# Attention and a routed expert layer: block rows issued two steps ahead, the first two blocks turned by TensorE, q's norms as a row

## The chip, the cores and the metric

One core of a Trainium2 chip runs the whole program. The metric is device time in microseconds (us) of one execution, taken as the median of several runs. A separate execution was recorded by the hardware profiler; its page and trace are what the argument reads. Engines: TensorE (PE, with its weight load PEld), VectorE (DVE), ScalarE (ACT), GpSimd (POOL) and SyncE (SP). SP and POOL each issue DMAs from a queue of their own, in order.

## The reference

Four batches of 5056 tokens with 256 channels go through an attention over channels, and all 20224 tokens then through a layer of eight experts of which each token takes one. The core of it:

```python
qn = q / (np.linalg.norm(q, axis=1, keepdims=True) + 1e-06)     # q, k, v: [4, 5056, 256]
kn = k / (np.linalg.norm(k, axis=1, keepdims=True) + 1e-06)
s = kn.transpose(0, 2, 1) @ qn / tau                             # [4, 256, 256]
a = softmax(s)                                                   # along the last axis
x = (v @ a).reshape(20224, 256)

logits = x @ w_gate + modality_bias[modality_id]                 # 8 experts
e_idx = argmax(logits); gate_w = softmax(logits)[e_idx]
for e in range(8):
    mask = e_idx == e
    out[mask] = gate_w[mask, None] * (np.maximum(x[mask] @ w1[e], 0) @ w2[e])   # 256 -> 1024 -> 256
```

The norms run over the tokens, one for each channel. Which expert a token goes to is known only on the chip.

## The kernel before

The program goes through 40 steps (`g`, ten for each batch, 512 tokens each; the last of a batch has 448) and 40 blocks (`slot`, up to 512 tokens of one expert each).

*Scores.* `kq_pieces` (line 265) loads q and k of a step and adds up k^T q in two PSUM tiles (`g0`, `g1`). The squares of q and k go by ScalarE, and VectorE adds them into `acc`, in two halves of 512 columns (line 347). Batch 0 is done ahead of everything; the pieces of the next batch run among the steps of the present one.

*Softmax.* `norms` (line 401), once in each batch, sums the squares over the partitions: eight products with a column of ones (line 409), which give the norms as columns. ScalarE takes the root, VectorE adds 1e-6 and takes the reciprocal. Those of k scale rows, so a column serves (`rk`). Those of q scale columns and are needed as a row in each partition: VectorE scales a unit matrix by them (`dq`), and a product with ones (line 435) spreads the row into PSUM (`rq`). `soft` then scales, takes the exponential and normalizes, and `turn_weights` and `gate_weights` make the weights `ah`, `al` that a step multiplies v with.

*Steps.* `va_pieces` (line 568) turns v, multiplies (`xp`, line 633), routes (`route`, line 639) and scatters the 512 rows into a table `xs` in device memory, ordered by expert, with four indirect DMAs of POOL's queue (line 529). Each row has its channels, its gate and its token's number.

*Blocks.* After a step, `pick` chooses an expert with a full block of rows. `block_pieces` (line 771) has what is to be done for it: `load_x` (line 777) reads the first row's number and fetches the rows (`xr`) by four DMAs of POOL's queue, a quarter of the channels each, in runs of 64 numbers, and the gates and numbers (`gt`) by a fifth. They depend on all scatters up to the step after which the block was chosen. `load_w` fetches the expert's weights in two halves, by SP's queue; `split_w` splits them, in four parts, into a rounded part and the rest (ScalarE's copy, VectorE's difference). `tr_x` (line 840) turns the rows: VectorE transposes squares of 32x32 (line 563), which with the order of the four quarters gives the whole turn, and then rows are split in the same way into `xh` and `xl`. `m1` (`hp`, line 861), a relu (`hh`, `hl`), `m2` (`y`, line 879) and `finish` (`yo`) follow, and four indirect DMAs of POOL scatter the results (line 529).

*Order.* The pieces of a step, of a block and of the next batch's scores are interleaved by `_interleave` (line 20), and a scheduler then sets each engine's order by its own estimate; the engines carry it out in that order. In the main loop (line 1012) a block chosen after step `gg` runs at `g` where `gg <= g - lag(g)`, with a lag of 4 that falls to 3; its loads (rows and weights together, the pieces under `"load"`) are issued at the start of the step before, and its rows are turned and its first weights split (`"prep"`) in the latter half of the block before. Block 0 is the first to run, at step 6. The rows' tiles have two buffers, the weights' three.

## Time and profile before

| | |
|---|---|
| time, median of 3 runs | 1216.53 us (1212.48 to 1221.39) |
| the profiled execution's own time | 1214.25 us |
| its span, first to last instruction | 1212.6 us |
| TensorE busy | 1175.0 us, 97% |
| VectorE, ScalarE, GpSimd busy | 879.8, 730.1 and 508.8 us |
| mean granted clock of TensorE | 0.986 |
| moved by DMA | 210.78 MB, 174 GB/s |

The profile's page gives busy time by engine, forty slices of the span with TensorE's granted clock, groups of instructions by line, and DMA issues. Its trace answers questions about single stretches. In a row of a timeline stand the start in us, the length in us, engine, line, operation, output<-inputs and count; a bracket tells how long the engine was idle before it and what ended that ("issue": nothing that the profile shows). In a row of windows stand the stretch, its length, the busy time of PE, PEld, DVE, ACT and POOL, the granted clock, the DMA engines' busy share and GB/s. A time of 1 us is 0.08% of the whole.

### The profile page before, as it was taken

Reading aid. Unit: us, or ns where it says so; the run is one execution under the profiler, and the core shown is the slowest. Engines: PE = TensorE matmul, PEld = TensorE weight load, DVE = VectorE, ACT = ScalarE, POOL = GpSimd, SP = SyncE. Lnnn points to the kernel's source line nnn. Section 1 sums busy time; section 2 is a strip of 40 time slices with the busy share of each in tenths; the row PEclk is TensorE's granted clock in tenths of the full one; section 3 lists DMA queues with packets and bytes.
Section 4 is the critical chain, followed back from the end, with each engine's and each line's share of the span. In section 5 each row is a group of like instructions: output and inputs, shape, how many; then the busy total and the mean of one; then the engine's idle time right before and its main releaser. Section 6 shows DMA issues by size and latency. Waiting matters only on the chain.

```text
span 1212.6 us, 22887 instructions
## 1 busy us (share of the span) xinstructions
PE 1175.0 (97%) x7654; PEld 1065.2 (88%) x7654; DVE 879.8 (73%) x2199; ACT 730.1 (60%) x1447; POOL 508.8 (42%) x544
## 2 busy tenths in 40 slices
PE   9996998999999999999989998999999999999997
PEld 8985987899999998998879997999999999999997
DVE  5697788887777877877678877766676677676552
ACT  6674586866666666676556665556555555554553
POOL 0057454325344444444434444333445344555432
PEclk9998998999999999999989998999999999999999
DMA  8977687557555666655656665554556554555430
GB/s 310 327 241 190 194 228 196 170 175 209 173 175 166 185 185 189 178 169 173 176 143 192 186 174 155 155 142 136 148 154 182 162 171 124 147 161 152 117 112 29
DMA packets 172399, 210.78 MB, mean 174 GB/s; under 512 B 80584, under 2 KB 126152, under 8 KB 172272
## 3 DMA queue, kind: packets, MB, share of 16 engines
q1 hardware_dynamic: 147632, 146.75, 41.7%
q0 software_dynamic: 24640, 62.49, 17.0%
q8 instruction: 62, 1.02, 0.4%
q14 instruction: 65, 0.53, 0.1%
HBM read 167.06 MB, written 43.43 MB: 174 GB/s over the span
## 4 chain that ended last, share of the span: by engine, by line
PE 44%; issue 3%; DVE 1%; DMA 1%; POOL 1%; POOLq 0%; ACT 0%; DVEq 0%; ACTq 0%
PE y L879 19%; PE hp L861 19%; PE xp L633 4%; PE g L370 1%; DMA xr<-xs 1%; PE g L374 1%; POOL out_dram L529 0%; DMA gt<-xs 0%; DVE hl L865 0%; DVE vt L563 0%; DVE w1l L836 0%; PE ns L409 0%; DVE xt L563 0%; PE rp L672 0%; POOLq L1062 0%
## 5 line engine op out<-in xcount | busy, mean ns | idle before, releaser
L529 POOL DMA_INDIRECT xs<-x,pi x160 | 184.9, 1155 | 463.1 <-ACT w1h L829 138.6
L879 PE MATMUL y<-w2h,hh 128*128 128x256 f32 x1264 | 357.6, 283 | 0.6 <-ACT yo L894 0.6
L879 PE MATMUL y<-w2l,hh 128*128 128x256 f32 x1264 | 354.9, 281 | 0.0
L879 PE MATMUL y<-w2h,hl 128*128 128x256 f32 x1264 | 352.9, 279 | 0.1
L861 PE MATMUL hp<-xh,w1h 128*128 128x512 f32 (+1 forms) x640 | 251.3, 393 | 3.4 <-DVE hl L865 3.4
L861 PE MATMUL hp<-xl,w1h 128*128 128x512 f32 (+1 forms) x640 | 253.3, 396 | 0.0
L865 DVE SCALAR_TENSOR_TENSOR hl<-hp,hh 128x512 fp32r<-128x512 f32 (+1 forms) x320 | 216.9, 678 | 50.2 <-ACT hh L864 49.2
L861 PE MATMUL hp<-xh,w1l 128*128 128x512 f32 (+1 forms) x640 | 251.8, 393 | 0.0
L879 PEld LDWEIGHTS y<-w2h,hh 128*128 128x128 f32 x1264 | 239.0, 189 | 13.5 <-ACT yo L894 1.0
L879 PEld LDWEIGHTS y<-w2l,hh 128*128 128x128 f32 x1264 | 239.4, 189 | 10.7
L864 ACT ACTIVATE hh<-hp 128x512 fp32r<-128x512 f32 (+1 forms) x320 | 189.6, 592 | 85.2 <-PE hp L861 76.5
L879 PEld LDWEIGHTS y<-w2h,hl 128*128 128x128 f32 x1264 | 238.2, 188 | 1.3 <-issue 0.9
L529 POOL DMA_INDIRECT out_dram<-yo,gt x158 | 172.2, 1090 | 149.6 <-ACT yo L894 106.3
L836 DVE TENSOR_TENSOR w1l<-w1r,w1h 128x512 fp32r<-128x512 f32 x160 | 110.2, 689 | 132.4 <-ACT w1h L829 132.4
L829 ACT CAST w1h<-w1r 128x512 fp32r<-128x512 f32 x160 | 99.2, 620 | 155.6 <-PE hp L861 155.3
L861 PEld LDWEIGHTS hp<-xh,w1l 128*128 128x128 f32 x640 | 121.2, 189 | 28.2 <-issue 2.9
L836 DVE TENSOR_TENSOR w2l<-w2r,w2h 128x512 fp32r<-128x512 f32 x160 | 110.1, 688 | 48.5 <-ACT w2h L829 45.9
L861 PEld LDWEIGHTS hp<-xl,w1h 128*128 128x128 f32 x640 | 121.3, 190 | 17.8 <-issue 4.2
L861 PEld LDWEIGHTS hp<-xh,w1h 128*128 128x128 f32 x640 | 121.1, 189 | 17.5 <-DVE hl L865 3.8
L783 POOL DMA_DIRECT2D xr<-xs x160 | 107.5, 690 | 52.6 <-DMA xs<-x,pi 22.2
L829 ACT CAST w2h<-w2r 128x512 fp32r<-128x512 f32 x160 | 100.5, 629 | 42.1 <-PE y L879 42.1
L633 PE MATMUL xp<-ah,vh 128*128 128x264 f32 x320 | 92.5, 289 | 2.1 <-DVE vl L610 1.0
(158 smaller groups left out, 1804.1 us busy)
## 6 DMA issues: line engine op xcount, KB each, us to landing
w1r<-in_moe_w_dram SPq DMA_DIRECT2D x80, 512.0 KB, 4.8
w2r<-in_moe_w_dram SPq DMA_DIRECT2D x80, 512.0 KB, 6.0
xr<-xs POOLq DMA_DIRECT2D x152, 128.0 KB, 3.6
q<-in_q_dram SPq DMA_DIRECT2D x35, 512.0 KB, 4.2
k<-in_k_dram SPq DMA_DIRECT2D x35, 512.0 KB, 5.3
v<-in_v_dram SPq DMA_DIRECT2D x112, 128.0 KB, 6.0
v<-in_v_dram SPq DMA_DIRECT2D x8, 512.0 KB, 10.3
xs<-x,pi POOLq DMA_INDIRECT x160, 3.6
```

The source lines that it names most:

```text
L370: nc.tensor.matmul(g, ks[:pp, t, m * P : (m + 1) * P], qs[:pp, t, :], start=first, stop=False, skip_group_check=True,)
L374: nc.tensor.matmul(g[:, 0:C], ks[:pp, t, C + m * P : C + (m + 1) * P], qs[:pp, t, 0:C], start=False, stop=last, skip_group_check=True,)
L529: ins = nc.gpsimd.indirect_dma_start(out=dst, out_offset=bass.IndirectOffsetOnAxis(ap=idx, axis=0), in_=rows, in_offset=None, bounds_check ...
L633: nc.tensor.matmul(xp[:, 0:DE], a[:, h, t * P : (t + 1) * P], w[:, h, :], start=i == 0, stop=i == len(seq) - 1,)
L783: nc.gpsimd.dma_start(xr[j * Q : (j + 1) * Q, 0 : rows // Q, :], src[:, j * CQ : (j + 1) * CQ].rearrange("(i t) c -> t i c", t=Q),)
L829: ins = nc.scalar.copy(hi, src).ins
L836: nc.vector.tensor_tensor(lo, src, hi.bitcast(F32), ALU.subtract)
L861: nc.tensor.matmul(hp[:, 0:rows], w[:, h, fs], x[:, h, 0:rows], start=i == 0, stop=i == len(seq) - 1)
L864: nc.scalar.activation(hh[:, 0:rows], hp[:, 0:rows], AF.Relu)
L865: nc.vector.scalar_tensor_tensor(hl[:, 0:rows], hp[:, 0:rows], 0.0, hh[:, 0:rows].bitcast(F32), ALU.max, ALU.subtract)
L879: ins = nc.tensor.matmul(y, a[:, tsl], w[:, j % 2, :], start=(j == 0 and i == 0 and t % 2 == 0), stop=(j == NJ - 1 and i == 2), skip_group ...
```

## The change

Four things are changed.

1. A block's rows are a piece of their own (`"rows"`, apart from `"load"`), issued up to two steps ahead of the block's run instead of one, after the first blocks. For block 0 they stand between the two halves of its weights.
2. The rows of blocks 0 and 1 (`WHOLE_ROWS`) are fetched by one DMA of SP's queue, whole rows of 256 numbers, with the gates by a second.
3. TensorE turns the rows of these two blocks by products with a unit matrix (`identr`, `xtp`), one PSUM tile for each half of the channels; ScalarE and VectorE split them from there. The other blocks are turned by VectorE as before.
4. `norms` adds the halves of `acc` first (VectorE). One product of a full matrix of ones with q's sums gives them as a row in every partition, and two small products give k's as columns, into the same tile. Root, 1e-6 and reciprocal run over all 258 columns; the scaled unit matrix and its product are gone.

```diff
-            ns = ps2.tile([P, 512], F32, tag="aux", name=f"ns_{b}")
-            for m in cols:
-                for h in range(2):
-                    cs = slice(m * P, (m + 1) * P) if m < CH else slice(C + m - CH, 2 * C, CH)
-                    nc.tensor.matmul(
-                        ns[:, m : m + 1], a[:, h, cs], ones[:, 0:1],
-                        start=m == cols[0] and h == 0, stop=h == 1, skip_group_check=True,
-                    )
...
-            dq = p1.tile([P, CH, P], F32, tag="at", name=f"dq_{b}")
-            for m in range(CH):
-                nc.vector.tensor_scalar(dq[:, m, :], ident, inv[:, m : m + 1], None, ALU.mult)
-            rq = ps2.tile([P, 512], F32, tag="aux", name=f"rq_{b}")
-            nc.tensor.matmul(rq[:, 0:C], ones, dq.rearrange("p m c -> p (m c)"), start=True, stop=True)
-            st["rq"] = rq
+            nc.vector.tensor_tensor(a[:, 0, :], a[:, 0, :], a[:, 1, :], ALU.add)
+            W = C + CH
+            ns = ps2.tile([P, 512], F32, tag="aux", name=f"ns_{b}")
+            nc.tensor.matmul(ns[:, 0:C], ones, a[:, 0, 0:C], start=True, stop=True, skip_group_check=True)
+            for m in range(CH):
+                nc.tensor.matmul(
+                    ns[:, C + m : C + m + 1], a[:, 0, C + m : 2 * C : CH], ones[:, 0:1],
+                    start=False, stop=True, skip_group_check=True,
+                )
+            inv = p1.tile([P, W], F32, tag="at", name=f"inv_{b}")
+            root = nc.scalar.activation(inv, ns[:, 0:W], AF.Sqrt).ins
...
+            st["rq"] = inv
...
-            r = nc.gpsimd.value_load(pki[0:1, 0:1], min_val=0, max_val=E * CAP)
-            xr = st["xr"] = p2.tile([P, QI, CQ], F32, tag="xr", name=f"xr_{slot}")
+            eng = nc.sync if slot < WHOLE_ROWS else nc.gpsimd
+            r = eng.value_load(pki[0:1, 0:1], min_val=0, max_val=E * CAP)
+            if slot < WHOLE_ROWS:
+                xr = p2.tile([P, TT, D], F32R, tag="xr", name=f"xr_{slot}")
+            else:
+                xr = p2.tile([P, QI, CQ], F32, tag="xr", name=f"xr_{slot}")
...
+                eng.dma_start(xr[:, 0:tt, :].bitcast(F32), src[:, 0:D].rearrange("(t p) c -> p t c", p=P))
+            ] if slot < WHOLE_ROWS else [
...
+            if slot < WHOLE_ROWS:
+                tp = ps2.tile([P, 512], F32R, tag="aux", name=f"xtp_{slot}_{h}")
+                for t in range(tt):
+                    nc.tensor.matmul(
+                        tp[:, t * P : (t + 1) * P], st["xr"][:, t, h::CH], identr,
+                        is_transpose=True, start=t == 0, stop=True, skip_group_check=True,
+                    )
+                raw, hi, lo = tp[:, 0:rows].bitcast(F32), xh[:, h, 0:rows], xl[:, h, 0:rows]
...
-        prep = [load_x, lambda: load_w(0), lambda: load_w(1)]
+        prep = [lambda: load_w(0), lambda: load_w(1)]
+        ahead = [load_x]
         if slot == 0:
 
-            prep[0:2] = reversed(prep[0:2])
-        prep2 = [lambda: split_w(0), tr_x, lambda: None, lambda: split_w(1)]
+            prep, ahead = prep[:1] + ahead + prep[1:], []
+        prep2 = [lambda: split_w(0), lambda: tr_x(0), lambda: tr_x(1), lambda: split_w(1)]
...
         for gg, blk in waiting:
+            n = 2 if g > first_block + WHOLE_ROWS else 1
+            if gg <= g + n - lag(g + n):
+                once(blk, "rows")
+        for gg, blk in waiting:
             if gg <= g + 1 - lag(g + 1):
                 once(blk, "load")
```

Since a scheduler sets the orders, the diff alone does not tell where the instructions stand. In the rows below a name is followed by its block or step, and then by a buffer's number; `pki` is the block's choice, of which the first row's number is read.

The first place is SP's queue at the first two blocks. Before:

```order
L806 DMA w1r_0_0_1179<-in_moe_w1_dram 128x2x512
L810 DMA w2r_0_0_1180<-in_moe_w2_dram 128x4x256
L806 DMA w1r_0_1_1199<-in_moe_w1_dram 128x2x512
L810 DMA w2r_0_1_1200<-in_moe_w2_dram 128x4x256
L802 TENSOR_LOAD pki_1_1028
L806 DMA w1r_1_0_1371<-in_moe_w1_dram 128x2x512
L810 DMA w2r_1_0_1372<-in_moe_w2_dram 128x4x256
L584 DMA v_8_1341<-in_v_dram 32x16x64 x4
```

The same place on SP now:

```order
L800 DMA w1r_0_0_1173<-in_moe_w1_dram 128x2x512
L804 DMA w2r_0_0_1174<-in_moe_w2_dram 128x4x256
L775 DMA xr_0_1186<-xs_129 128x4x256
L783 DMA gt_0_1187<-xs_129 128x4x2
L800 DMA w1r_0_1_1190<-in_moe_w1_dram 128x2x512
L804 DMA w2r_0_1_1191<-in_moe_w2_dram 128x4x256
L775 DMA xr_1_1356<-xs_129 128x4x256
L571 DMA v_8_1342<-in_v_dram 32x16x64 x4
L783 DMA gt_1_1357<-xs_129 128x4x2
L796 TENSOR_LOAD pki_1_1022
L800 DMA w1r_1_0_1369<-in_moe_w1_dram 128x2x512
```

Both blocks' rows stand on SP now, those of block 0 ahead of the second half of its weights, and those of block 1 ahead of a load of v and of its own weights. On TensorE, after the last product of step 5, stood before:

```order
L633 MATMUL xp_5_3_1245<-ah_0_482,vl_5_1035 128x264
L604 MATMUL vtp_7_0_1428<-ident_79,v_7_1168 128x128 x4
L604 MATMUL vtp_7_1_1460<-ident_79,v_7_1168 128x128 x4
L633 MATMUL xp_6_0_1507<-ah_0_482,vh_6_1203 128x264
L633 MATMUL xp_6_0_1507<-al_0_483,vh_6_1203 128x264
```

and now there stands on TensorE:

```order
L620 MATMUL xp_5_3_1236<-ah_0_476,vl_5_1029 128x264
L844 MATMUL xtp_0_0_1300<-identr_84,xr_0_1186 128x128 x4
L844 MATMUL xtp_0_1_1307<-identr_84,xr_0_1186 128x128 x4
L868 MATMUL hp_0_0_1377<-xh_0_1298,w1h_0_0_1289 128x512
L868 MATMUL hp_0_1_1392<-xh_0_1298,w1h_0_0_1289 128x512
```

Block 0's turn and first products come directly after step 5, and the turn of step 7's v and the products of step 6 after them. The second place is POOL at the rows of block 4, before:

```order
L783 DMA xr_4_2592<-xs_127 32x16x64
L529 DMA xs_127<-x_7_1392,pi_7_2052 168448x258 x4
L529 DMA out_0_dram<-yo_1_2201,gt_1_1356 20224x256 x4
L783 DMA xr_4_2592<-xs_127 32x16x64
L789 DMA gt_4_2593<-xs_127 128x4x2
```

The first of these rows is the last of three issues; now, on POOL:

```order
L777 DMA xr_4_2600<-xs_129 32x16x64
L783 DMA gt_4_2601<-xs_129 128x4x2
L516 DMA xs_129<-x_7_1390,pi_7_2060 168448x258 x4
L516 DMA out_0_dram<-yo_1_2209,gt_1_1357 20224x256
L766 TENSOR_LOAD pki_5_2113
```

All four issues (the first row here is the last of them) now stand ahead of the scatters of step 7 and of block 1's results. The third place is POOL at the rows of block 18, before:

```order
L529 DMA xs_127<-x_21_7505,pi_21_8159 168448x258 x4
L778 TENSOR_LOAD pki_18_8212
L783 DMA xr_18_8655<-xs_127 32x16x64
L529 DMA out_0_dram<-yo_15_8308,gt_15_7329 20224x256 x4
L783 DMA xr_18_8655<-xs_127 32x16x64
L789 DMA gt_18_8656<-xs_127 128x4x2
```

and now, on POOL:

```order
L516 DMA xs_129<-x_21_7513,pi_21_8167 168448x258 x4
L766 TENSOR_LOAD pki_18_8220
L777 DMA xr_18_8242<-xs_129 32x16x64
L783 DMA gt_18_8243<-xs_129 128x4x2
L516 DMA out_0_dram<-yo_15_8316,gt_15_6923 20224x256 x4
```

The scatters of block 15's results stood between the first and the other three issues and now stand behind all four. At block 22 POOL's order is the same in both: step 25's scatters, those of block 19's results, a memset of a padding tile, then the rows. On VectorE the turns (`xt`) of blocks 2, 3, 4, 5, 10, 19 and 35 stand earlier by one to five pieces `hl` (there are eight in a block), those of blocks 6 and 16 later by three and one; the others stand where they stood among them.

57 lines of the change are left out of this document (29 added, 28 removed).

## The prediction

> **What bounds the kernel now.** I read the page first: the busy shares, the clock in slices, the DMA issues.
>
> ```profile
> PE 1175.0 (97%) x7654; PEld 1065.2 (88%) x7654; DVE 879.8 (73%) x2199; ACT 730.1 (60%) x1447; POOL 508.8 (42%) x544
> PEclk9998998999999999999989998999999999999999
> q<-in_q_dram SPq DMA_DIRECT2D x35, 512.0 KB, 4.2
> w2r<-in_moe_w_dram SPq DMA_DIRECT2D x80, 512.0 KB, 6.0
> xs<-x,pi POOLq DMA_INDIRECT x160, 3.6
> ```
>
> TensorE is busy 97% of a span of 1212.6 us, so 37.6 us are idle and only that, slow clock, or TensorE's own work can be won. The clock shows a few slices below 9 or 10 tenths. The list of TensorE's waits says where the idle time lies (us in total, times, longest):
>
> ```profile
> PE rp L672 <- DVE sm L692: 7.9, 2, 4.1
> PE g L374 <- DVE ks L322: 7.9, 1, 7.9
> PE hp L861 <- DVE hl L865: 3.4, 2, 2.0
> PE rp L672 <- DVE x L696: 2.9, 1, 2.9
> ```
>
> All of them wait for VectorE, though VectorE is busy only 73%. So the next view was VectorE's timeline at those places; four of its rows open them:
>
> ```profile
> 106.05 1.25 DVE L563 STREAM_TRANSPOSE xt<-xr 128x1024 f32<-128x1024 f32 x1 [6.72 <-DMA xr<-xs]
> 182.59 1.25 DVE L563 STREAM_TRANSPOSE xt<-xr 128x1024 f32<-128x1024 f32 x1 [3.94 <-DMA xr<-xs]
> 605.15 1.25 DVE L563 STREAM_TRANSPOSE xt<-xr 128x1024 f32<-128x1024 f32 x1 [5.17 <-DMA gt<-xs]
> 727.70 1.25 DVE L563 STREAM_TRANSPOSE xt<-xr 128x1024 f32<-128x1024 f32 x1 [4.28 <-DMA xr<-xs]
> ```
>
> The bracket is VectorE's idle time: each time it stands at the turn of a block's rows (blocks 0, 4, 18 and 22, by the count of such rows) until they land, with the pieces TensorE wants queued behind. Each wait also costs clock; windows of 10 us from the end of each TensorE wait (us, busy of PE, PEld, DVE, ACT, POOL, then the granted clock):
>
> ```profile
> 108.05:118.05 10.00, 10.00 (x42) 8.47 (x43) 8.28 (x13) 5.26 (x10) 8.25 (x11) 0.77 0.56 120
> 189.55:199.55 10.00, 10.00 (x50) 8.70 (x51) 7.62 (x27) 7.10 (x14) 5.20 (x4) 0.75 0.41 115
> 611.88:621.88 10.00, 10.00 (x49) 8.66 (x49) 6.23 (x22) 4.34 (x11) 3.68 (x4) 0.71 0.43 151
> 732.52:742.52 10.00, 10.00 (x55) 9.08 (x55) 7.04 (x25) 4.99 (x12) 3.78 (x4) 0.76 0.43 133
> ```
>
> TensorE is busy throughout, at 0.71 to 0.77 of the clock: 2.3, 2.5, 2.9 and 2.4 us lost. With the waits, the places at blocks 4, 18 and 22 cost 3.8 + 2.5 = 6.3, 2.0 + 2.9 + 2.9 = 7.8 and 4.1 + 2.4 = 6.5 us (7.9 and 3.4 split by the longest in each row). Why the rows are late is in POOL's timeline:
>
> ```profile
> 81.53 0.98 POOL L529 DMA_INDIRECT xs<-x,pi  x1 [0.30 <-issue]
> 89.43 0.72 POOL L783 DMA_DIRECT2D xr<-xs  x1 [6.92 <-issue]
> 95.67 1.40 POOL L783 DMA_DIRECT2D xr<-xs  x2
> 102.78 0.72 POOL L783 DMA_DIRECT2D xr<-xs  x1
> ...
> 152.26 0.66 POOL L783 DMA_DIRECT2D xr<-xs  x1 [1.50 <-issue]
> 177.09 0.73 POOL L783 DMA_DIRECT2D xr<-xs  x1
> ...
> 585.94 0.98 POOL L529 DMA_INDIRECT xs<-x,pi  x1 [0.31 <-issue]
> 591.85 0.71 POOL L783 DMA_DIRECT2D xr<-xs  x1 [4.93 <-DMA xs<-x,pi]
> 597.92 2.04 POOL L783 DMA_DIRECT2D xr<-xs  x3
> ...
> 718.94 2.68 POOL L783 DMA_DIRECT2D xr<-xs  x4 [2.76 <-issue]
> ```
>
> Two causes. The first issue of a block's four waits until the last scatter has landed (585.94 to 591.85). And scatters stand between the four: block 0's last is issued 13.35 us after its first, block 4's 24.8 us after its third, block 18's last three 6.1 us after its first. Block 22's four stand together and are late as a whole.
>
> **The change, part by part.** *Block 0.* Its rows go by one DMA of SP's queue, and its turn leaves VectorE. The views that size it are TensorE's timeline, at its first transposes after the last step that both orders share and at the first product of the second layer, and a window over the place:
>
> ```profile
> 91.29 1.38 PE L604 MATMUL vtp<-ident,v 128*128 128x128 f32 x8
> 113.94 0.28 PE L879 MATMUL y<-w2h,hh 128*128 128x256 f32 x1
> 90.00:113.00 23.00, 12.18 (x63) 9.94 (x62) 14.90 (x53) 10.23 (x24) 19.34 (x21) 0.78 0.73 190
> ```
>
> From 91.29 to 113.94 are 22.65 us; 10.8 of the window's 23 are idle on TensorE and 2.3 go to the clock, which leaves 9.5 us of work. In the new order TensorE comes to the rows at 91.29. The rows can be issued when step 2's scatters have landed, by 88.7 (89.43 less POOL's own issue); with the 4.2 us of a 512 KB load they are there at 92.9. The bound on the other side: the second half of block 0's weights now stands behind these rows on SP, so the scatters have the DMA engines more to themselves, and at their usual 3.6 us from 81.53 the rows are there at 89.3, before they are wanted. Then TensorE needs 9.5 us and 1.1 for transposes: 102. VectorE has 14.9 us of work in the window less the turn's 1.25, from 90: 103.7. VectorE decides, and the new way from transposes over ScalarE's copy and VectorE's difference to the first product adds about 1.5 us that nothing covers: 105 to 106.5 in place of 113.94. I take 7.5 us won; 9 if VectorE's work fits without gaps, 2 if the wait moves (first rival below).
>
> *What SP now holds.* Behind block 0's rows stand their gates, the other half of block 0's weights, and then block 1's rows, which wait for step 3's scatters, with four loads of v and block 1's weights behind them. ScalarE's copy of those second-half weights stands ahead of block 0's first relu, and VectorE's ahead of step 5's routing. With 6.0 us to land, from about 90, they are there at 96 to 97, when the first two products of block 0 are just done: I take nothing, with the rival as the other end.
>
> *Block 4.* All four issues of its rows now stand ahead of step 7's and block 1's scatters: issued about 25 us earlier by the rows above, so that the wait of 3.94 is gone. 6.3 us at most; VectorE is what is late next, so I take 5.
>
> *Block 18.* The four issues stand ahead of the scatters of block 15's results. The first keeps its time, 591.85, since the landing it waits for is the same; the other three follow at once (2.0 us for three), by 594 in place of 600. The turn began at 605.15, 5.17 of it idle, so the rows are wanted at 600 and would land at 599. 7.8 us at most, I take 7.
>
> *Block 22 and the rest.* The order on POOL there is the same: scatters of step 25, of block 19's results, the memset, then the rows. Nothing for it. For most other blocks the rows move ahead of one to three scatters but still wait for the same landing, and no TensorE wait hangs on them.
>
> *Norms.* TensorE's timeline at the first softmax and at a step's turn of v, the groups on VectorE, and the rows that show the cover:
>
> ```profile
> 42.73 1.89 PE L409 MATMUL ns<-ones,acc 128*128 128x1 f32 x16
> 58.20 1.12 PE L604 MATMUL vtp<-ident,v 128*128 128x128 f32 x8
> L347 DVE TENSOR_TENSOR acc<-acc,sq_k 128x512 f32<-128x512 f32 x68 | 46.6, 686 | 4.3 <-ACT sq_k L345 3.0
> L455 DVE TENSOR_SCALAR ae<-sc,ssm 128x256 f32<-128x256 f32 x8 | 2.9, 369 | 0.0
> L426 DVE TENSOR_SCALAR inv<-inv 128x4 f32<-128x4 f32 x4 | 0.7, 167 | 3.6 <-ACT inv L416 3.6
> L427 DVE RECIPROCAL inv<-inv 128x4 f32<-128x4 f32 x4 | 0.7, 174 | 0.0
> 53.31 0.17 DVE L502 TENSOR_TENSOR al<-gw,ah 128x16 fp32r<-128x16 f32 x1 [0.41 <-ACT ah L499]
> 55.18 0.37 PE L633 MATMUL xp<-ah,vh 128*128 128x264 f32 x1
> ```
>
> Sixteen instructions (eight products in two passes) take 1.89 us, 0.118 each. Four remain (0.47). The product of ones that spread q's norms goes and one of the same shape comes. That is 1.4 us of TensorE a batch, 5.7 in four, all of it in full stretches. Against it stand sixteen transposes for blocks 0 and 1; eight for v take 1.12, so 2.2. Net 3.5 won. On VectorE a sum of 128x512 comes in (0.69), and the reciprocal grows from 4 columns to 258. Its price lies between the 0.37 of a tensor_scalar over 256 columns and 0.82: over 4 columns it takes 7 ns more than the addition, 1.75 a column, 0.45 for 258. I take 0.6, and 0.2 more each for the wider root and addition, 1.7 with the sum. Against that the softmax loses 1.4 us of sums and the trip over q's scaled unit matrix. In batch 0 the weights are ready at 53.48 for a product at 55.18, a cover of 1.7; if the losses won nothing and the cover were gone, it would be 1.7 us, once. I count nothing.
>
> [...] TensorE's transposes at 58.20 stand among products, so this trace does not show what the clock does on transposes after a wait. [...]
>
> **The sum.** The profiled execution took 1214.25 us (span 1212.6 and 1.65 around it). 1214.25 - 7.5 - 5 - 7 - 3.5 = 1191.25. The median of the runs, 1216.53, is 2.3 above the profiled one: 1193.5, so 1194.
>
> **The rivals.** *The wait moves to SP's weights.* If step 2's scatters land at 88.5 as before and each transfer takes its 6 us in a row, block 0's second weights land near 101, and the relus behind them wait. For it: SP runs its queue in order; against it: less traffic ahead of the scatters. Block 0 then wins 2: 1199.
>
> *Rows that cannot come earlier.* The earlier place on POOL buys nothing while a landing is awaited, and blocks 4 and 18 wait again for another reason. For it: 4.93 us at 591.85 were a landing. Against: the late issues were those behind other scatters. 1194 + 5 + 7 = 1206.
>
> [...]
>
> *Block 22 mends itself too,* because the memset or POOL's 2.76 us fall elsewhere: 1194 - 6.5 = 1187.
>
> *VectorE meets rows too early.* In the new order the turns of blocks 2, 3, 4, 5, 10, 19 and 35 stand earlier on VectorE. Where rows land as late as before, VectorE stands at the turn as it did for block 22, 6.5 us each. All seven give 46: 1240; with four it is 1220 and from there on slower than before. Against it: for blocks 3 to 5 the order issues the rows well ahead of the turn too.
>
> **How the numbers follow.** The forecast 0.52 (1188 to 1200 alone), SP's weights 0.10, late rows 0.14, the clock 0.06, block 22 mended 0.11, VectorE too early 0.07. About 1% (12.2 us, a limit at 1204.4) is what a measurement of this kernel can tell from no change. Faster by over 1% take the forecast, weights, clock, block 22: 0.79, less some spread of waits between runs (1212 to 1221 before), and a third of the late rows: 0.77. Within 1%: 0.16. Slower: 0.07. The range 1184 to 1210 leaves out part of block 22's case and VectorE's.
>
> **What would show it.** Block 0: no VectorE wait over 2 us at 90 to 110, the first y near 105. Blocks 4 and 18: four row issues together, no bracket at the turn, full clock in the slices there. Block 22 still waits about 4 us. Norms: 24 instructions in place of 72 for the sums and q's row, TensorE's total about 3.5 us lower beyond the clock. It is wrong if TensorE's list of waits has new rows over 3 us behind a weight copy, or if turns of blocks 3, 5, 10 or 19 show brackets.

## The result and the profile after

The changed kernel takes 1179.9 us (median of four runs, 1179.17 to 1183.62) against 1215.53 for the kernel before (four runs, 1212.48 to 1221.39): a ratio of 0.9707, 95% interval 0.9665 to 0.975. The forecast was 1194 with a range of 1184 to 1210. The direction is right, the gain is 13 us larger than the sum had it, and the time lies below the range. The profiled execution took 1179.17 us with a span of 1177.4, 35.1 us less than before (35.2 by the spans), and the rest of this section asks where they came from.

The page of the kernel after, its busy shares and its clock in slices:

```profile
PE 1161.6 (99%) x7622; PEld 1054.6 (90%) x7622; DVE 880.7 (75%) x2196; ACT 730.5 (62%) x1449; POOL 506.2 (43%) x534
PEclk9999999999999999999999999999999999999999
```

TensorE's idle time is 15.8 us in place of 37.6, and the four dips of the clock are gone. By the trace's rows of the clock, TensorE lost 10.1 us to it while busy before, and none now; what is left, its work at full clock, is 1165.0 us before and 1161.6 after. So the 35.2 us are 21.8 of idle time, 10.1 of clock and 3.4 of work. The list of TensorE's waits in the kernel after (us in total, times, longest):

```profile
PE hp L868 <- DVE hl L872: 1.8, 2, 1.6
PE g L359 <- DMA k<-in_k_dram: 1.4, 2, 0.7
PE hot L946 <- DVE keep L123: 1.3, 1, 1.3
PE rp L659 <- DVE x L683: 1.2, 2, 0.6
```

Before, four rows with totals of 2.9 to 7.9 us headed this list; now no total reaches 2 us. VectorE's timeline in the kernel after, at the turns of the rows of blocks 4, 18 and 22:

```profile
150.40 1.24 DVE L550 STREAM_TRANSPOSE xt<-xr 128x1024 f32<-128x1024 f32 x1
579.03 1.24 DVE L550 STREAM_TRANSPOSE xt<-xr 128x1024 f32<-128x1024 f32 x1
695.75 1.25 DVE L550 STREAM_TRANSPOSE xt<-xr 128x1024 f32<-128x1024 f32 x1
```

No row has a bracket where before there stood 3.94, 5.17 and 4.28 us: at all three the rows are there first, at block 22 too. POOL's timeline at the issues of blocks 4, 18 and 22:

```profile
134.72 2.65 POOL L777 DMA_DIRECT2D xr<-xs  x4
...
572.93 2.67 POOL L777 DMA_DIRECT2D xr<-xs  x4 [5.78 <-DMA xs<-x,pi]
...
689.88 2.68 POOL L777 DMA_DIRECT2D xr<-xs  x4 [1.31 <-issue]
```

The four issues of blocks 4 and 18 now stand together (x4), as the order said. Block 22's did before as well, with 2.76 in that bracket in place of 1.31. SP's timeline has what goes out next to it, the second half of block 22's first-layer weights, first in the kernel before and then in the kernel after:

```profile
719.55 0.56 SPq L806 DMA_DIRECT2D w1r<-in_moe_w_dram  x1
...
691.94 0.56 SPq L800 DMA_DIRECT2D w1r<-in_moe_w_dram  x1
```

POOL's first issue (718.94 before, 689.88 after) was 0.61 us ahead of it before and is 2.06 ahead now. For block 0, SP's timeline and TensorE's:

```profile
75.97 0.65 SPq L800 DMA_DIRECT2D w1r<-in_moe_w_dram  x1
76.81 0.45 SPq L804 DMA_DIRECT2D w2r<-in_moe_w_dram  x1
84.20 0.39 SPq L775 DMA_DIRECT2D xr<-xs  x1
84.80 0.37 SPq L783 DMA_DIRECT2D gt<-xs  x1
85.42 0.57 SPq L800 DMA_DIRECT2D w1r<-in_moe_w_dram  x1
```

```profile
89.95 1.39 PE L844 MATMUL xtp<-identr,xr 128*128 128x128 f32 x8
91.28 0.74 PE L868 MATMUL hp<-xh,w1h 128*128 128x512 f32 x2
...
96.18 0.38 PE L886 MATMUL y<-w2h,hh 128*128 128x256 f32 x1
```

The rows are issued at 84.20, and TensorE turns them at 89.95 without a wait; the first product of the second layer stands at 96.18, where before it stood at 113.94. Not all of these 17.8 us are a gain: before, step 6's products and step 7's turn stood ahead of it, and most of that work now stands behind. Windows of us over the place in the kernel after (busy of PE, PEld, DVE, ACT, POOL, granted clock, DMA share, GB/s):

```profile
87.00:110.00 23.00, 22.16 (x141) 19.46 (x141) 21.49 (x74) 16.22 (x35) 13.61 (x14) 1.00 0.91 265
88.66:96.18 7.52, 6.88 (x40) 5.47 (x38) 6.49 (x27) 5.83 (x15) 4.44 (x4) 1.00 0.72 207
```

TensorE was busy 12.2 us of 23 at 0.78 of the clock; it is now busy 22.2 of 23 at full clock. From the first transposes of the table below to block 2's first product, TensorE was idle for 10.8 us before and lost 2.3 to the clock; now it is idle for 0.9 and loses none.

How much each place gave can be read without any model: in each timeline every block has 48 first-layer products, so the start of each block's first one is a mark that both traces share. The gain is the difference of the marks, and where it grows, something was won:

```
start of the first hp product of block    before    after    gain   grown by
(V's transposes at 91.29, same work)       91.29    89.95    1.34   1.3   norms, batch 0
2                                         157.51   146.45   11.06   9.7   blocks 0 and 1
3                                         195.34   177.81   17.53   6.5   block 4's rows
5                                         259.47   240.49   18.98   1.5   norms, batch 1
14                                        515.27   495.97   19.30   0.3
15                                        547.46   526.88   20.58   1.3   norms, batch 2
18                                        642.38   614.71   27.67   7.1   block 18's rows
21                                        727.29   699.68   27.61   0
22                                        761.99   728.00   33.99   6.4   block 22's rows
25                                        847.82   812.64   35.18   1.2   norms, batch 3
39                                       1184.95  1149.78   35.17   0
```

Four places and the four small steps of the norms make the whole. Between them the two traces run in parallel to within 0.3 us, but for blocks 16 and 17, where the gain is 19.95 and 21.57.

### The profile page after: what moved, and what is told of

Same layout as the page of the kernel before. It is cut to its first block, busy times and chain, and to the rows that moved or that the text cites. A ratio compares the mean times of both kernels' runs of the same rounds, so it can differ in the third digit from the quotient of the medians.

```text
span 1177.4 us, 22795 instructions
## 1 busy us (share of the span) xinstructions
PE 1161.6 (99%) x7622; PEld 1054.6 (90%) x7622; DVE 880.7 (75%) x2196; ACT 730.5 (62%) x1449; POOL 506.2 (43%) x534
## 4 chain that ended last, share of the span: by engine, by line
PE 86%; DMA 4%; issue 3%; DVE 3%; ACT 2%; POOL 1%; POOLq 0%; SPq 0%; DVEq 0%; ACTq 0%
PE y L886 34%; PE hp L868 34%; PE xp L620 8%; PE g L359 4%; PE g L373 3%; PE g L377 2%; DMA k<-in_k_dram 2%; DMA w2r<-in_moe_w_dram 1%; DMA xr<-xs 1%; DMA xs<-x,pi 0%; POOL out_dram L516 0%; DVE acc L350 0%; DMA q<-in_q_dram 0%; PE vtp L591 0%; DVE hl L872 0%
## 5 line engine op out<-in xcount | busy, mean ns | idle before, releaser
L516 POOL DMA_INDIRECT out_dram<-yo,gt x158 | 178.3, 1128 | 146.9 <-ACT yo L901 102.5
L777 POOL DMA_DIRECT2D xr<-xs x152 | 101.9, 683 | 75.0 <-DMA xs<-x,pi 45.0
L868 PEld LDWEIGHTS hp<-xh,w1h 128*128 128x128 f32 x640 | 120.0, 188 | 15.8 <-DVE hl L872 2.1
L624 ACT COPY x<-xp 128x264 f32<-128x264 f32 x160 | 60.7, 381 | 58.1 <-PE xp L620 57.5
```

The source lines that it names most:

```text
L516: ins = nc.gpsimd.indirect_dma_start(out=dst, out_offset=bass.IndirectOffsetOnAxis(ap=idx, axis=0), in_=rows, in_offset=None, bounds_check ...
L624: nc.scalar.copy(st["x"][:, t, :], xp[:, 0:DE])
L777: eng.dma_start(xr[j * Q : (j + 1) * Q, 0 : rows // Q, :], src[:, j * CQ : (j + 1) * CQ].rearrange("(i t) c -> t i c", t=Q),)
L868: nc.tensor.matmul(hp[:, 0:rows], w[:, h, fs], x[:, h, 0:rows], start=i == 0, stop=i == len(seq) - 1)
```

## The experiments

Two theories stood at the start. Mine, from the table: block 0 gains because SP brings its rows early, blocks 4 and 18 because their issues stand together, and block 22 by something that the order does not show. The rival: the parts only shift the program in time, and the waits fall away by luck of which transfer comes first.

**The kernel before once more.** No edit.

> The kernel before, unchanged, profiled once more. If block 22's wait belongs to the kernel's order, VectorE's bracket at that turn is again near 4.3 us, POOL's first issue again about 4.5 us ahead of the moment the rows are wanted, and the time is 1212 to 1221 us. If it was an accident of the one profiled execution, the bracket is under 1 us and the time about 6 us below 1214. In both cases the brackets at blocks 0, 4 and 18 stand as before (6.7, 3.9 and 5.2 us).

It took 1216.84 us (one run). VectorE's brackets at blocks 0, 4, 18 and 22, in its timeline:

```profile
105.50 1.25 DVE L563 STREAM_TRANSPOSE xt<-xr 128x1024 f32<-128x1024 f32 x1 [6.83 <-DMA xr<-xs]
183.42 1.25 DVE L563 STREAM_TRANSPOSE xt<-xr 128x1024 f32<-128x1024 f32 x1 [6.07 <-DMA xr<-xs]
607.92 1.25 DVE L563 STREAM_TRANSPOSE xt<-xr 128x1024 f32<-128x1024 f32 x1 [7.58 <-DMA gt<-xs]
729.38 1.25 DVE L563 STREAM_TRANSPOSE xt<-xr 128x1024 f32<-128x1024 f32 x1 [3.85 <-DMA xr<-xs]
```

All four are back, with sizes that differ by up to 2.4 us from the first profile. Block 22's wait belongs to the kernel before and was no accident of one execution.

**The norms alone.** The kernel before, with the function norms() of the kernel after; its core:

```diff
-            for m in cols:
-                for h in range(2):
...
-                        ns[:, m : m + 1], a[:, h, cs], ones[:, 0:1],
...
+            nc.vector.tensor_tensor(a[:, 0, :], a[:, 0, :], a[:, 1, :], ALU.add)
...
+            nc.tensor.matmul(ns[:, 0:C], ones, a[:, 0, 0:C], start=True, stop=True, skip_group_check=True)
```

> The kernel before with the new norms and nothing else. My sum: 1.4 us of TensorE for each batch, all in full stretches: 5.7 us less than before, brackets at blocks 0, 4, 18 and 22 unchanged. Rival one, the longer sum on VectorE and the wider root are not covered: 2 to 4 us less. Rival two, the shift in time alone changes which transfer comes first at block 22 and its bracket goes: about 12 us less.

1208.59 us (eight runs), ratio 0.9951 (0.9934 to 0.9969), so 6.0 us less, 3.8 to 8.0: my sum of 5.7. The marks of its trace grow by 1.6, 1.3 and 1.2 at batches 1 to 3. Batch 0's share does not arrive: at block 0's first product it is 0.3 behind the kernel before, since the wait for the rows (bracket 6.75) swallows it. The second rival does not hold, for block 22's bracket stays (3.13), and the first one's 2 to 4 only touches the lower end of the interval.

**Blocks 0 and 1 alone.** The kernel after, with norms() of the kernel before, and one more line:

```diff
-            n = 2 if g > first_block + WHOLE_ROWS else 1
+            n = 1
```

> The kernel before with blocks 0 and 1 alone changed: rows through SP between the halves of the weights, turned by TensorE; all other rows as far ahead as before, old norms. On POOL block 4's four issues now stand together here too, block 18's stand apart as before. From the trace after: block 0 gains 9.7 us net of the transposes and block 4 gains 6.5: 16 us less than before, and block 18 keeps its 5 us bracket. By the sizes of the prediction: 5.3 and 5, about 10 less. If block 4 needs its rows a step earlier: 9.7 less, with the bracket of 3.9 still there. If block 22's wait hangs on when things happen, it may be gone here too: 6.5 more.

1203.98 us (four runs), ratio 0.9914 (0.9887 to 0.9942): 10.5 less, where the trace's sizes promised 16, and 22.5 with block 22. The marks settle why. At block 2 the gain is 10.3, and 16.8 at block 3: blocks 0 and 4 are mended in full by this part alone. It was then partly lost again: VectorE's bracket at block 18 is 8.15 in place of 5.17, between the marks of blocks 19 and 20 4.0 us go, and at batches 1, 2 and 3 it loses 1.4, 1.4 and 1.7 us. POOL's timeline at block 18 shows the issues apart as before:

```profile
578.63 0.72 POOL L793 DMA_DIRECT2D xr<-xs  x1 [5.52 <-DMA xs<-x,pi]
579.65 1.01 POOL L532 DMA_INDIRECT out_dram<-yo,gt  x1 [0.30 <-ACT qs L324]
...
585.40 2.05 POOL L793 DMA_DIRECT2D xr<-xs  x3
```

And block 22's wait is gone here (6.4 us by the marks), with the same order on POOL around it as before. So the mending needs neither the rows issued two steps ahead nor the new norms.

**Two steps ahead alone.** The kernel after, with norms() of the kernel before, and no block set apart:

```diff
-    WHOLE_ROWS = 2
+    WHOLE_ROWS = 0
-            n = 2 if g > first_block + WHOLE_ROWS else 1
+            n = 2 if g > first_block + 2 else 1
```

> The kernel before with rows issued two steps ahead from block 7 on, alone: blocks 0 and 1 and the norms as before. Block 18's four issues stand together ahead of the scatters, block 4's still apart. My sum: block 18 gains 7, everything else as before: 7 us less (6 to 7.8), brackets at blocks 0, 4 and 22 unchanged. If the earlier issues of blocks 7 to 21 are what mended block 22: 13 to 14 less. If nothing comes earlier because the same landing is awaited: no change.

1207.45 us (ten runs, 1199.2 to 1212.66), ratio 0.9941 (0.9915 to 0.9967): 7.2 less (4.0 to 10.3), the 7 of my sum in number, but not in its parts. In its profile block 18's bracket is 0.71, its mark grows by 6.1, block 4's wait (5.42) stays, and block 22's bracket is 0.28 with 6.1 won there. That profiled execution took 1202.36, five below the median; which of the two the slower executions lack is not recorded.

**Is it the number of POOL's instructions?** In the sequencer's rows of the traces, POOL's step from preparing block 22's first row issue to the issue takes 1.86 us in the kernel before and 0.59 in the kernel after. Other such stops of about 1.3 us extra lie some 163 recorded rows, or 50 to 52 DMA preparations, apart; the change moves them off block 22 to the second issue of block 20 and the first of block 24. The next run tries to move them in the kernel before.

```diff
         nc.gpsimd.memset(pad[0], 0.0)
+        for _ in range(41 if name == "pad0" else 0):
+            nc.gpsimd.memset(room[:, 0:1], 0.0)
```

> The kernel before with 41 extra one-column memsets on POOL while it is idle at the start; nothing else. In the three profiles with the old order on POOL the step from the first row of block 22's issue to the next takes 1.84 us where others take 0.55; such stops of POOL's stream lie some 163 rows of the trace apart. Theory: the stop goes with the number of instructions, so it now falls about one block earlier, block 22's first issue comes 1.3 us earlier against the moment the rows are wanted, ahead of the second half of the weights on SP, and VectorE's bracket there (4.3 us) goes: about 6 us less than before; blocks 0, 4 and 18 as before. Rival one: the stop goes with something else (the DMAs), stays at block 22, and nothing changes. Rival two: the stop moves but the rows are late all the same: no change.

1214.6 us (ten runs), ratio 0.9996 (0.9972 to 1.0019). The stop stands where it stood, 41 instructions later in the stream: rival one. Block 22's bracket is 2.60 in this profile.

**A later issue in the kernel after, first try.**

```diff
+            late = [nc.gpsimd.memset(room, 0.0).ins for _ in range(10 if slot == 22 else 0)]
...
+            for ins in late:
+                order(ins, written[g])
             for ins in moved:
+                order(ins.ins, late)
```

> The kernel after with ten memsets of 120 columns on POOL in front of block 22's rows: its first issue comes 1 to 2 us later. If the bracket at block 22 comes from the place of the issue against SP's weights, it is back at 3 to 5 us with a clock loss behind it, and the run is 4 to 7 us longer than the 1179.9 of after. If the rows have more slack than that, or if the change mended something else, the bracket stays under 1 us and the time is unchanged.

1180.59 us: no change. Half of the memsets fell between POOL's scatters, and the issue led the weights by 1.62 us in place of 2.06, with a bracket of 0.66, although VectorE came to the rows 7.0 us behind the issue in place of 5.9. The delay was smaller than the 1 to 2 us that it was to be.

**Block 0's rows behind both halves of its weights.**

```diff
-            prep, ahead = prep[:1] + ahead + prep[1:], []
+            prep, ahead = prep + ahead, []
```

> The kernel after with both halves of block 0's weights ahead of its rows on SP, the rest unchanged. If the 1 MB of the second half slows step 2's scatters, as in the trace before, they land near 87 in place of 83.8, the rows near 92, and TensorE waits 3 to 4 us at block 0's transposes: 3 to 6 us longer than after, the 7.5 of the prediction in place of what was gained. If the scatters land early anyway, the time is that of after.

1183.7 us (1181.2 to 1187.12), 3.8 above after's median and 3.1 above the run with memsets beside it; the intervals of the ratios overlap (0.9685 to 0.9795 and 0.9661 to 0.9764), and the marks do not put the difference at block 0. SP's timeline and TensorE's:

```profile
78.38 0.39 SPq L804 DMA_DIRECT2D w2r<-in_moe_w_dram  x1
86.04 0.38 SPq L775 DMA_DIRECT2D xr<-xs  x1
```

```profile
91.07 1.29 PE L844 MATMUL xtp<-identr,xr 128*128 128x128 f32 x8 [0.95 <-DMA xr<-xs]
```

With the megabyte ahead step 2's scatters land 1.8 us later, as I held (the rows go out at 86.04 in place of 84.20), and TensorE waits 0.95 us for it; the mark at block 2 is 0.6 behind after. The rest lies elsewhere: 2.3 us between the marks of blocks 3 and 5, where the clock is at half for 3.4 us behind a wait of 1.69 at 210, and 1.2 at block 22, where VectorE waits 1.21 us with a lead of 1.88. So the place of the rows on SP is worth under 1 us at block 0, not the 4.4 by which I was short.

**Rows one step ahead, with all else changed.**

```diff
-            n = 2 if g > first_block + WHOLE_ROWS else 1
+            n = 1
```

> The kernel after with rows issued one step ahead everywhere: blocks 0 and 1 and the norms stay as changed. On POOL block 18's issues stand again apart around four scatters, block 4's four stay together. Theory: only block 18's bracket returns (5 to 8 us) with its clock: 6 to 8 us longer than after; block 22 stays mended, since the stop of POOL's stream stays away from it. If the earlier issue is what mended block 22, its bracket is back too: 12 to 14 longer.

1193.57 us (four runs), ratio 0.9819 (0.9766 to 0.9873): 13.7 above after. Block 18's bracket is back (4.09), and from block 15's mark to its own the run loses 7.5 us against after; block 22's bracket is 0.20. The theory has the right brackets and the right size at block 18, but the whole is more than its 6 to 8: 3.0 us are lost by block 1's mark, 0.8 more by block 5's and 1.2 at block 20, places that the part was not known to touch.

The ten runs that follow come from two other chips, on both of which every kernel takes about 3% longer, the kernel before 1247 to 1250 us. Where a run was made twice, it was made once on each. The kernel after itself ran on one of them. On the other, the run with fourteen memsets and the one with 25 DMAs stand in for it (1218.33 and 1218.6 us): by their ratios to the kernel before, 0.9758 and 0.978, they are level with after's 0.9768.

**The kernel after once more, on a slower chip.** No edit.

> The kernel after, unchanged, as the measure for the three beside it: 1178 to 1184 us where the kernel before takes 1215. If block 22's mending was an accident of the one profiled execution, VectorE's bracket there is back at 2.5 to 4.5 us in this profile; if it belongs to the order, it is under 1 us again.

1219.19 us (four runs, 1215.21 to 1222.38), ratio to the kernel before 0.9768 (0.972 to 0.9815). That is 28 us less than the kernel before, where the first chips gave 35.6. Block 22's bracket is 0.41: the mending belongs to the changed kernel.

**A later issue, second try,** twice. Fourteen memsets in place of ten, all else as in the first try:

```diff
+            late = [nc.gpsimd.memset(room, 0.0).ins for _ in range(14 if slot == 22 else 0)]
...
+            for ins in late:
+                order(ins, written[g])
             for ins in moved:
+                order(ins.ins, late)
```

> The kernel after with fourteen memsets of 120 columns on POOL in front of block 22's rows. With ten the first issue came 1.62 us ahead of the second half of block 22's weights on SP in place of 2.06, and VectorE's bracket was 0.66 us. The four more add about 1.03 us (0.257 each), so the issue leads by about 0.6 us, as it did in the kernel before (0.61 and 0.78 us, brackets 4.3 and 2.6). If that lead decides, the bracket is 2.5 to 4.5 us here and TensorE waits 2.4 to 4.1 us: 2 to 6 us longer than the 1180.6 of the run with ten. If the lead is not the cause, the bracket grows by no more than the 1 us of the delay.

> The kernel after with fourteen memsets of 120 columns on POOL in front of block 22's rows, so that their first issue leads the second half of its weights on SP by about 0.6 us instead of 2.06. If the lead decides: VectorE's bracket 2.5 to 4.5 us, TensorE waits 2 to 4 us and may lose clock, 2 to 6 us longer than after beside it. If not: the bracket stays under 1.1 us, and the time is that of after.

1218.33 and 1217.06 us, level with after. The lead over the weights was 0.86 us, about as wished, and the bracket 0.01 and 0.00. But VectorE's own order had moved with the memsets: it asked for the rows 7.8 us behind the issue, where it is 5.9 in after and 4.5 in before. So the time decides nothing on the lead. The rows themselves do: in the trace's DMA packets, the last packet of block 22's rows ends 6.9 us behind POOL's first issue in both runs, where it is 5.1 in the kernel after and 7.5 in the kernel before. With the shorter lead the rows come later, though POOL has no stop there; VectorE came later still.

**The old norms in the changed order,** twice. The kernel after, with norms() of the kernel before; its core:

```diff
-            nc.vector.tensor_tensor(a[:, 0, :], a[:, 0, :], a[:, 1, :], ALU.add)
...
-            nc.tensor.matmul(ns[:, 0:C], ones, a[:, 0, 0:C], start=True, stop=True, skip_group_check=True)
...
+            for m in cols:
+                for h in range(2):
```

> The kernel after with the norms of the kernel before: the whole change but for its third part. By the prediction's sum 5.7 us longer than the 1179.9 of after. If the sixteen one-column products cost clock here as in the run with the first two blocks alone, where the clock fell to half for 3.4 us at two of the four batches without any wait of TensorE over 0.5 us beside them: 8 to 10 us longer, with half-clock rows of 3.4 us at batches 1 to 3.

> The kernel after with the norms of the kernel before. By the prediction's sum 5.7 us longer than after beside it. If the one-column products also cost clock in this order, as at two batches of the run with the first two blocks alone: 8 to 10 us longer, with half-clock stretches of 3.4 us at the batches.

1223.2 and 1224.01 us: 4.6 to 4.9 above the two runs that stand in for after on the first's chip, and 4.8 above after beside the second, whose interval of the ratio, 0.9766 to 0.9879, overlaps with after's. The 5.7 of the sum fits. An extra cost in clock shows in one of the two profiles: the second has the mean clock of after beside it, 0.989, and the first, itself 3.4 us above its median, has 0.982, with 3.4 us at half clock from 522.0, 1.2 us behind the one-column products of batch 2. How much of its other lost clock is theirs is not shown.

**Blocks 0 and 1 turned by VectorE,** twice. Their rows still go by SP, in quarters as the others.

```diff
+    TURNED_PE = 0
...
-            if slot < WHOLE_ROWS:
+            if slot < TURNED_PE:
                 tp = ps2.tile([P, 512], F32R, tag="aux", name=f"xtp_{slot}_{h}")
```

> The kernel after with the rows of blocks 0 and 1 still by SP between the halves of the weights, but in quarters and turned by VectorE as all others: the sixteen transposes leave TensorE. If the early rows alone made block 0's gain, TensorE saves the 2.2 us of transposes and the time is 0 to 2 us shorter than after's 1179.9. If VectorE's turn standing in its queue was half of the matter, as the prediction had it, TensorE waits 2 to 5 us at block 0 and the time is 2 to 6 us longer, with clock lost.

> The kernel after with the rows of blocks 0 and 1 by SP in quarters and turned by VectorE: the sixteen transposes leave TensorE. If the early rows alone made block 0's gain: 0 to 2 us shorter than after beside it. If the turn standing in VectorE's queue was half of the matter: TensorE waits 2 to 5 us at block 0, 2 to 6 us longer than after, with clock lost. On the other chip it was level with after's ratio (0.9713 to 0.9707), so 0 to 1 us longer is likeliest.

1211.41 and 1216.04 us, ratios 0.9713 (0.9684 to 0.9742) and 0.9747 (0.9701 to 0.9792). The second is 3.2 us below after beside it, with intervals that overlap, and the first 7 below the two runs that stand in for after on its chip: not slower, and by the medians the fastest on both of these chips. VectorE's turn of block 0 in the second of them:

```profile
100.72 1.25 DVE L551 STREAM_TRANSPOSE xt<-xr 128x1024 f32<-128x1024 f32 x1
```

No bracket: the rows came first. Against after beside it this second run is 1.8 us behind at block 2's mark and 1.4 ahead at block 3's. Block 0's gain does not need TensorE's transposes.

**Rows of blocks 0 and 1 by POOL, in one DMA each, turned by TensorE.**

```diff
-            eng = nc.sync if slot < WHOLE_ROWS else nc.gpsimd
+            eng = nc.gpsimd
```

> The kernel after with the rows of blocks 0 and 1 by POOL in one DMA each, turned by TensorE: SP now has both halves of the weights ahead of step 2's scatters' landing, and POOL holds step 3's scatters behind block 0's rows. If SP is what makes the rows early: step 2's scatters land near 86 as with the rows behind the weights, block 0's rows are 1 to 2 us late, step 3's scatters 3 to 5 us later, and block 1 or 2 waits: 2 to 6 us longer than after. If one DMA in place of four scattered ones is all that counts: within 1.5 us of after.

1230.44 us (1228.72 to 1231.94), 12 above the two runs that stand in for after on this chip, twice what was expected at most. POOL's timeline, TensorE's, and a window from TensorE's last product ahead of its wait:

```profile
84.79 0.98 POOL L516 DMA_INDIRECT xs<-x,pi  x1 [0.30 <-issue]
91.98 0.83 POOL L775 DMA_DIRECT2D xr<-xs  x1 [6.22 <-issue]
92.80 0.79 POOL L783 DMA_DIRECT2D gt<-xs  x1
93.89 1.56 POOL L516 DMA_INDIRECT xs<-x,pi  x1 [0.30 <-ACT w2h L823]
...
104.52 0.81 POOL L775 DMA_DIRECT2D xr<-xs  x1 [5.09 <-DMA xs<-x,pi]
```

```profile
100.59 1.34 PE L844 MATMUL xtp<-identr,xr 128*128 128x128 f32 x8 [5.63 <-DMA xr<-xs]
```

```profile
94.90:104.90 10.00, 4.25 (x16) 3.44 (x16) 4.18 (x20) 3.87 (x10) 3.99 (x5) 0.76 0.92 249
```

POOL stands idle for 6.22 us ahead of block 0's rows (the row names no releaser; by the order they wait for step 2's landing) with step 3's scatters behind them, then 5.09 for step 3's landing with step 4's behind; TensorE waits 5.63 at the transposes, and the clock falls (0.76 in the window). With the run before, this settles block 0: it is the queue that brings the rows, not their number of DMAs and not the engine that turns them. What it does not part is the queue's two effects: the scatters held behind the rows, and SP's second half of the weights, which now goes out ahead of step 2's landing (1.8 us later for that alone in the run with the rows behind the weights).

**Moving POOL's stop by DMAs,** 13 in the kernel before, and in the same place 25 in the kernel after:

```diff
+        for i in range(13 if name == "pad0" else 0):
+            nc.gpsimd.dma_start(room[:, 4 * i : 4 * i + 4], wg[0:P, 0:4])
```

> The kernel before with 13 loads of 2 KB each on POOL at the start, into a tile that nothing reads. If the stop of POOL's stream goes with the DMAs it has issued, it now falls 13 DMAs earlier, at block 21's first issue; block 22's first issue then leads the second half of its weights by about 2 us in place of 0.6, VectorE's bracket of 2.6 to 4.3 us there goes, and the time is 2 to 6 us less than before. If the stop does not go with the DMAs, it stands at block 22 as before and nothing changes.

> The kernel after with 25 loads of 2 KB each on POOL at the start, into a tile that nothing reads. In after the stop stands at block 24's first issue, 25 DMAs behind block 22's first. If the stop goes with the DMAs and block 22's wait with the stop: POOL's step there takes 1.84 us, the issue leads the weights by about 0.7 us, the bracket is back at 2.5 to 4.5 us and the run is 3 to 6 us longer than after. If the stop comes and the bracket does not, something else mended block 22. If the stop stays at block 24, the time is that of after.

1249.1 us, ratio 1.001 (0.9984 to 1.0035): the stop stays at block 22 (step 1.89) with a bracket of 3.95. 1218.6 us, ratio 0.978, level with after's 0.9768: here the stops did move, from block 24's first issue to block 23's, and not onto block 22. VectorE's turns of block 24 in after and of block 23 here have no bracket; the leads there are 2.49 and 2.75 us even with the stop. What sets the stops' place was not found. The profiles can still be laid side by side; per kernel, POOL's idle bracket at block 22's first issue, by how much that issue leads the second half of block 22's first-layer weights on SP, how long after the issue VectorE comes to the rows, when the last packet of the rows ends after it, and VectorE's bracket (us):

```
kernel                          POOL bracket   lead   wanted after   last packet   VectorE bracket
before                                  2.76   0.61           4.49          7.46              4.28
before once more                        2.77   0.60           4.48          7.50              3.85
norms alone                             2.57   0.80           4.68          6.79              3.13
before, 41 memsets                      2.60   0.78           4.65          6.33              2.60
before, 13 DMAs                         2.60   1.00           4.87          7.51              3.95
blocks 0 and 1 alone                    1.30   2.07           5.88          5.30              0.00
two steps ahead alone                   1.30   2.07           5.95          5.72              0.28
one step ahead, rest changed            1.30   2.07           5.95          5.53              0.20
after                                   1.31   2.06           5.87          5.14              0.00
after once more                         1.31   2.10           5.98          5.46              0.41
after, rows behind weights              1.49   1.88           5.75          6.25              1.21
after, 10 memsets                       0.60   1.62           6.99          6.79              0.66
after, 14 memsets                       0.60   0.86           7.83          6.90              0.01
```

In the first five rows POOL has the stop; in the last two the memsets fill its bracket. In the seven profiles that are not listed there is no stop at block 22 either; VectorE's bracket there is 0 to 0.22.

## Why the prediction was right or wrong

**Blocks 4 and 18: right.** 6.5 and 7.1 us for the 5 and 7 of the sum; both reached their ceilings of 6.3 and 7.8 to within a microsecond, and nothing came late behind them. The term of block 4 was 1.5 short, since I took off 1.3 for a VectorE that is late next, and it was not. The split, which the prediction did not give, is from the runs: block 4 comes from taking blocks 0 and 1 off POOL, block 18 from the second step ahead.

**Norms: right.** 1.3, 1.5, 1.3 and 1.2 us, 5.3 together for 5.7; alone 6.0 with an interval of 3.8 to 8.0, and 4.6 to 4.9 when taken out again. TensorE's work at full clock fell by 3.4 us, the 3.5 of the sum with the transposes. No wait shows for VectorE's longer sum.

**Block 0: the early rows right, the size wrong.** The term was 7.5, less 2.2 for the transposes: 5.3. The marks give 9.7. Two steps were mis-sized. One is the row's landing: I took 92.9, the far one of two bounds, and TensorE began on them at 89.95 without a wait, which is the near bound of 89.3 (the scatters, with SP's second half of the weights behind the rows, had landed by 84.2, when the rows were issued). The run with the rows behind the weights prices that step at 0.6 to 1 us, so it is the smaller one. The larger is "VectorE decides": I set all of VectorE's 13.65 us in the window ahead of the first product of the second layer and got 105. In the new order VectorE was busy only 6.49 us from the moment that answers to 90 (88.66) until that product began, at 96.18; the rest of its work stands behind. So does part of TensorE's: step 6's products and step 7's turn, which I counted in the 9.5 us ahead of that product, stood behind block 0's first products in the order that the change shows. And the 1.5 us for the way from the transposes to the first product was an estimate with no row behind it: the transposes stand at 89.95 for 1.39, that product at 91.28, with no gap. The moment of the first product of the second layer was therefore the wrong measure: it came 17.8 us earlier, and the gain is 9.7. What TensorE had to win there was its idle time and the clock, 10.8 + 2.3 us, less 2.2 for the transposes; 0.9 of it is left. A sum over a window bounds an engine's throughput, not the moment of one product, and the order, which could be read, told which of those instructions came first. The runs with VectorE's turn agree: putting the turn back on VectorE cost no time. "Its turn leaves VectorE" shows as no part of the gain, and the 16 transposes as a price with no return seen.

**Block 22: "Nothing for it" is the step that failed.** 6.4 us were won there. The rival "Block 22 mends itself too" had the right place and the right price, 1187 with the rest of the sum, and too low a chance at 0.11; with block 0's 4.4 and block 4's 1.5 on top, 1187 becomes 1181. What the runs show: in all five profiles in which POOL's step to block 22's first issue has 1.3 us extra, VectorE waits 2.6 to 4.3 us there; in the fifteen without it, 0 to 1.2. The wait has two parts. With the stop, the issue comes only 4.5 to 4.9 us ahead of the moment VectorE wants the rows, in place of 5.9. And the rows are longer on the way: their last packet ends 6.3 to 7.5 us behind the issue where it leads SP's next half megabyte by 0.6 to 1.0, and 5.1 to 5.9 where the lead is 2.06 or more. In after the first packet of that half megabyte starts 3.75 us behind POOL's first issue, in before 1.99, so the packets of both are on the way together for 1.4 us in after and for 5.5 in before. The memsets show that a shorter lead does this without a stop: at 1.62 the last packet ends at 6.8, at 0.86 at 6.9. The bracket told of it before: 2.76 "issue" at 718.94, in which POOL waited for nothing that the row names. I read it as a fixed cost of that place in the order, and an order that stays word for word the same says nothing on a stop that does not belong to it. No run moved the stop onto block 22 or off it at will, so its share in the wait is read from profiles laid side by side, and what sets its place stays open.

**The clock at block 0: did not come.** No slice and no window shows less than full clock there (1.00 from 87 to 110). The chance of 0.06 for it was my estimate, and no row of the kernel before stood behind it. In the run with the rows behind the weights TensorE waited 0.95 us ahead of eight transposes, 1.29 us together, and the clock did not fall; that is a weak test, since plain waits cost no clock either: 1.6 us in the kernel after, 2.15 in the second run with the old norms. With a wait of 5.63 us the clock did fall, to 0.76 in the window, but the waits of the kernel before cost clock before products too (0.71 to 0.77 in the prediction's four windows). Whether the transposes had a part in it no run tells.

**SP's weights, late rows, VectorE too early: none came.** No row of TensorE's waits names a weight copy, and the turns of blocks 3, 5, 10 and 19 have no bracket.

**The parts do not add up, and the sum did not say so.** 6.0 + 10.5 + 7.2 us for the parts alone are 23.7, and the whole is 35.6. That 23.7 meets my 23 is chance: in their profiles two of the parts hold block 22's 6 us, which my 23 had not, and blocks 0 and 1 alone lose 11.4 us elsewhere. Put on top of each other they do add up: blocks 0 and 1 alone bring 10.9 us (1203.98), the new norms 10.4 more (1193.57, the run one step ahead), the second step 13.7 more (1179.9). Alone, a part runs into what the others take away: the norms of batch 0 into block 0's wait, blocks 0 and 1 into a longer wait at block 18 and a loss of clock at the old norms.

## What to carry to other kernels

A wait that the profile puts down to a late transfer may hang on a lead of a microsecond over another queue (at block 22 the last packet ended 6.3 to 7.5 us behind the issue with a lead of 0.6 to 1.0, and 5.1 to 5.9 with 2.06 or more); before it is booked as a fixed cost or as none, ask how much later it is wanted than issued and what goes out next on the other queues. Rows that wait for a landing belong on a queue with nothing urgent behind the wait: the rows of two blocks cost 12 us more on POOL, ahead of the scatters, than on SP. And a busy sum over a window is an upper bound for throughput; when one product starts is read from the order of the instructions ahead of it (105 by the sum, 96.18 in the trace).

## What the hardware showed that I had not expected

**POOL's stops.** The 1.3 us extra between preparing a DMA and issuing it (1.86 us for 0.59 at block 22), some 50 to 52 preparations apart, stay at block 22 under 41 more memsets or 13 more small DMAs, and move with a change of the rows' order or 25 more DMAs.

**Half clock without a wait.** In the run with blocks 0 and 1 alone, TensorE's timeline around the sixteen one-column products of batch 2 and a window behind them:

```profile
502.21 1.97 PE L412 MATMUL ns<-ones,acc 128*128 128x1 f32 x16
504.05 0.37 PE L902 MATMUL y<-w2h,hh 128*128 128x256 f32 x1
...
505.99 0.63 PE L884 MATMUL hp<-xh,w1h 128*128 128x512 f32 x1
```

```profile
505.30:508.70 3.40, 3.40 (x11) 2.82 (x12) 3.24 (x20) 0.66 (x2) 1.04 (x1) 0.50 0.04 10
```

TensorE is busy throughout, and a microsecond behind the small products the clock is at 0.50 for 3.4 us (0.63 us for a product that takes 0.39). It happens at batches 2 and 3 of that run (0.50 from 809.1 to 812.5 at the second), at batch 2 of the kernel before with 41 memsets (from 518.1, with no wait near it) and of one run with the old norms (from 522.0), and at none of the two profiles of the kernel before itself, with the same instructions. What sets the length, and which batches it comes at, the runs do not show. That the one-column products bring it on is how I read these four places; no run tested it.

**One program, two chips.** On the slower chip the kernel after took 9.2 us more than on the first between its marks at blocks 14 and 15 alone, at the softmax of batch 2, where TensorE's timeline has

```profile
530.87 1.02 PE L475 MATMUL gw<-wg_sb,at 128*128 128x8 f32 x4 [6.04 <-ACT at L459]
```

a wait of 6.04 for a copy of ScalarE's that the first chip's trace does not have. ScalarE itself stood idle for 6.00 us ahead of that, ended by what its row calls only "remote"; such rows come to 33.8 us on ScalarE in this profile, and the first chip's has none. What lies behind them the profile does not tell.
